# Three W group buffers instead of two in a fused spectral-filter kernel, with the last-stage constants loaded in the drain and six shuffle buffers instead of eight

## The chip, the cores and the metric

The kernel runs on one core of a Trainium2 chip. The metric is device time in microseconds (us), from the start of an execution to its end. Executions of one kernel vary: TensorE's granted clock is halved for stretches whose place and length differ between executions. A run over 1.5% above the fastest run of the same kernel is labelled slow, the others fast. Ratios are the mean time of one kernel's fast runs over the mean of the other's fast runs of the same rounds, so they are not quite the ratio of the medians that are quoted beside them.

Engines: PE is the matrix engine (TensorE), ACT is ScalarE, DVE is VectorE, POOL is GpSimd, SP is SyncE, which here only issues transfers.

## The reference, cut to what matters

```python
def reference(A_x, A_w_r, A_w_i, B_x, B_w_r, B_w_i, gate_w):   # x: 1 x 2048 x 1024, w: 2048 x 513, bf16
    g = sigmoid((A_x * gate_w).sum(-1, keepdims=True))
    X = rfft2(A_x.astype(float32), axes=(-2, -1))
    a = irfft2(X * (A_w_r + 1j * A_w_i), s=(2048, 1024)).astype(bfloat16)
    b = irfft2(X * (B_w_r + 1j * B_w_i), s=(2048, 1024)).astype(bfloat16)    # the kernel uses A_x for both
    return g * a + (1 - g) * b
```

(The B branch is applied to A's x.)

## The kernel before: the parts that matter

The Fourier transforms are matrix products with constant tables. The 2048 rows are handled as 16 "quads" of 128 frequency rows, t = 0 to 15. Four quads share one group of filter weights W (2.1 MB), so there are four groups, loaded into two buffers. Each quad passes a chain over four engines: `f2` (PE, then ACT writes T), `f3` (PE, then ACT writes X), `cmul` (DVE, the product with W, gives Y), `i1` (PE, then ACT writes two tiles rl), and a *shuffle*: one transfer for each rl that lays its rows out anew for the last stage. Two quads, a pair, go through in each turn of the loop.

```python
    wp = ctx.enter_context(tc.tile_pool(name="wp", bufs=2))
    ...
    gw = const.tile([P, 1024], BF16, name="gw")                  # gate weights, read by the 16 gate sums
    ...
    IG = const.tile([P, 8, 512], BF16, name="ig")                # constants of the last stage, 1 MB
    ...
    def load_w(gr):
        w = wp.tile([P, 4, 4, MH], BF16, name="w", tag="w")
        ...  # 16 transfers (20 for group 0) of 128 KB, all on SyncE's queue
    nc.sync.dma_start(WF[:], dr["WF"]); load_w(0); nc.sync.dma_start(WI[:], dr["WI"]); load_w(1)
    nc.sync.dma_start(Ec[:], dr["E"]); nc.sync.dma_start(idb[:], dr["ID"])
    ...
    def zsum(s1):                                                # a gate sum, DVE
        junk = wk.tile([P, 1024], BF16, name="rl", tag="rl", bufs=8)
        nc.vector.scalar_tensor_tensor(out=junk[:], in0=x[:, s1, :], scalar=1.0, in1=gw[:], op0=ALU.mult,
                                       op1=ALU.mult, accum_out=z[:, s1:s1 + 1])
    ...
    def gate_weights(b):
        dg = wk.tile([P, 4, 128], BF16, name="dg", tag="dg", bufs=1)
        nc.gpsimd.tensor_tensor(dg[:], ...)                      # diagonal of gate values, GpSimd
        ...
    for u in range(NT // 2 + 1):
        if 2 * u < NT:
            f2(2 * u)
        if u >= 2:
            i1(2 * u - 4)
        if u >= 1:
            f3(u - 1)
        if 2 * u < NT:
            f2(2 * u + 1)
        if u >= 2:
            i1(2 * u - 3)
        if u >= 1:
            cmul(2 * u - 2)
            cmul(2 * u - 1, ...)
        if u == 2 or u == 4:
            load_w(u // 2 + 1)
        if u == 5:
            nc.sync.dma_start(IG[:], ...)
    ...
    i1(L - 1)                                                    # the drain: quads 14 and 15
    i1(L, (0,))
    i1(L, (1,))                                                  # shuffles of quad 15 go on SyncE's queue
    gate_weights(0)
    spin(24)                                                     # dummy matmuls before the tail
    ...                                                          # the tail: i2_part and i3 for 16 row blocks
```

Of the kernel before, what the change touches and what calls it, by code (L numbers as in the profile page):

```python
# [10 lines left out]
P = 128  # L11
S = 2048
D = 1024
MH = 513
NT = 16
NS1 = 16
BF16 = mybir.dt.bfloat16
# [24 lines left out]
def make_constants():  # L42
# [23 lines left out]
    FD = np.zeros((512, 2, 2, 256))  # L66
    IG = np.zeros((2, 2, 256, 512))
    for eo in range(2):
# [3 lines left out]
        FD[:, eo, 1] = -np.sin(ph)  # L72
        IG[eo, 0] = 2 * np.cos(ph).T
        if eo == 0:
            FD[:, 0, 1, 0] = np.cos(np.pi * d1)
            IG[0, 0, 0] = 1
        m = 2 * i + (2 if eo == 0 else 1)
        IG[eo, 1] = -2 * np.sin(2 * np.pi * np.outer(m, d1) / D)
        if eo == 0:
            IG[0, 1, 255] = np.cos(np.pi * d1)  # L80
    IG /= S * D
    c["FD"] = _bf16np(FD.reshape(4, 128, 2, 512).transpose(1, 2, 0, 3))
# [37 lines left out]
def kernel(ctx, tc, A_x, A_w_r, A_w_i, B_x, B_w_r, B_w_i, gate_w, out):  # L120
    nc = tc.nc
    cn = make_constants()
    dr = {n: nc.inline_tensor(a, name=f"cst_{n.lower()}").ap() for n, a in cn.items()}
# [2 lines left out]

    const = ctx.enter_context(tc.tile_pool(name="const", bufs=1))
    big = ctx.enter_context(tc.tile_pool(name="big", bufs=1))
    wp = ctx.enter_context(tc.tile_pool(name="wp", bufs=2))
    wk = ctx.enter_context(tc.tile_pool(name="wk", bufs=2))  # L130
    yp = tc.alloc_tile_pool(name="yp", bufs=1)
    pp = ctx.enter_context(tc.tile_pool(name="pp", bufs=3, space=bass.MemoryType.PSUM))
# [5 lines left out]
    def ptile():  # L138
        return pp.tile([P, 1024], F32, name="pt", tag="pt")
# [1 line left out]
    ctx.enter_context(tc.manual_schedule())  # L141
    F1 = const.tile([P, 2, 128], BF16, name="f1")
    nc.scalar.dma_start(F1[:].rearrange("p a b -> p (a b)"), dr["F1"])
    gw = const.tile([P, 1024], BF16, name="gw")
    g1 = wk.tile([P, 1024], BF16, name="rl", tag="rl", bufs=8)[0:1, :]
    nc.scalar.dma_start(g1, gate_w.rearrange("(a d) -> a d", a=1))
    ones = const.tile([P, 128], BF16, name="ones")
    nc.vector.memset(ones[:], 1.0)
# [12 lines left out]
    nc.sync.dma_start(FD[:], dr["FD"])  # L161
    WF = const.tile([P, NT, 3, 64], BF16, name="wf")
    WI = const.tile([P, NT, 3, 64], BF16, name="wi")
    IG = const.tile([P, 8, 512], BF16, name="ig")
    Ec = const.tile([P, 2, 128], BF16, name="ec")
    idb = const.tile([P, 128], BF16, name="idb")

# [2 lines left out]
    def load_w(gr):  # L170
        w = wp.tile([P, 4, 4, MH], BF16, name="w", tag="w")
        for a, src in enumerate((A_w_r, A_w_i, B_w_r, B_w_i)):
            for q, r0, dr_ in ((0, 8 * gr, 1), (2, 8 * gr + 4, 1), (1, 64 - 8 * gr, -1), (3, 60 - 8 * gr, -1)):
                c0 = 0
                if gr == 0 and q == 1:
                    nc.sync.dma_start(w[32:64, a, 0, :], bass.AP(src.tensor, 32 * MH, [[64 * MH, 32], [1, MH]]))
                    c0 = 1
                nc.sync.dma_start(w[32 * q:32 * q + 32, a, c0:4, :],  # L178
                                  bass.AP(src.tensor, (r0 + dr_ * c0) * MH, [[64 * MH, 32], [dr_ * MH, 4 - c0], [1, MH]]))
        Ws[gr] = w  # L180
# [8 lines left out]
    ps = ptile()  # L189
# [7 lines left out]
    g = const.tile([P, NS1], F32, name="g")  # L197

    def zsum(s1):
        junk = wk.tile([P, 1024], BF16, name="rl", tag="rl", bufs=8)  # L200
        nc.vector.scalar_tensor_tensor(out=junk[:], in0=x[:, s1, :], scalar=1.0, in1=gw[:], op0=ALU.mult,  # L201
                                       op1=ALU.mult, accum_out=z[:, s1:s1 + 1])

    zs = 0
    for s1 in range(NS1):
        ps = ptile()
        for q in range(4):
            for h in range(2):
                nc.tensor.matmul(ps[:, q * 256:(q + 1) * 256],  # L209
                                 lhsT=x[:, s1, h * 512 + q * 128:h * 512 + (q + 1) * 128],  # L210
                                 rhs=(bc(F1[:, 0, :]).to_broadcast([P, 2, 128]) if h == 0 else F1[:]),
# [28 lines left out]
    Ts, Xs, Ys = {}, {}, {}  # L240
# [12 lines left out]
    def f3(u):  # L253
        ts = (2 * u, 2 * u + 1)
        ps = {t: ptile() for t in ts}
        pl = {t: ps1.tile([P, 512], F32, name=n, tag=n) for t, n in zip(ts, ("pl", "pg"))}
        for r in range(2):
            for e, m in enumerate(((0, 2), (1, 0))[r]):
                for t in ts:
                    for h in range(2):  # L260
                        i_, o_ = slice(64 * h, 64 * h + 64), slice(64 * (h ^ (t & 1)), 64 * (h ^ (t & 1)) + 64)
                        nc.tensor.matmul(ps[t][o_, r * 512 + e:(r + 1) * 512], lhsT=WF[i_, t, m, :],  # L262
                                         rhs=Ts[t][i_, e, e:512], start=(e == 0), stop=(e == 1))
        for r in range(2):
            for t in ts:
                for h in range(2):
                    i_, o_ = slice(64 * h, 64 * h + 64), slice(64 * (h ^ (t & 1)), 64 * (h ^ (t & 1)) + 64)
                    nc.tensor.matmul(pl[t][o_, r:r + 1], lhsT=WF[i_, t, (2, 0)[r], :], rhs=Ts[t][i_, 1, 0:1],
                                     start=(r == 0), stop=(r == 1), skip_group_check=True)
        X = wk.tile([P, 2, 2, MH], BF16, name="X", tag="X")  # L270
        for t in ts:
            nc.scalar.copy(out=X[:, t & 1, :, 0:512], in_=ps[t][:].rearrange("p (r m) -> p r m", r=2))  # L272
            nc.vector.tensor_copy(out=X[:, t & 1, :, 512:513], in_=pl[t][:, 0:2].rearrange("p (r m) -> p r m", m=1))
            Xs[t] = X[:, t & 1]

    def cmul(t, parts=(slice(0, 2),)):
        X, w = Xs.pop(t), Ws[t // 4]
        p = wk.tile([P, 2, 2, MH], BF16, name="p", tag="p", bufs=1)
# [3 lines left out]
        for ab in parts:  # L282
            n = ab.stop - ab.start
            for r, o in ((0, Y), (1, p)):
                nc.vector.tensor_tensor(o[:, ab].rearrange("p a r m -> p (a r) m"),  # L285
                                        bc(X[:, r, :]).to_broadcast([P, 2 * n, MH]),
                                        wv[:, ab].rearrange("p a r m -> p (a r) m"), ALU.mult)
# [3 lines left out]
    def i1(t, parts=(0, 1)):  # L291
        Y = Ys[t]
        ps = {ab: ptile() for ab in parts}
        for e in range(2):
            for r, m in enumerate(((0, 2), (1, 0))[e]):
                for ab in parts:
                    for h in range(2):
                        i_, o_ = slice(64 * h, 64 * h + 64), slice(64 * (h ^ ab), 64 * (h ^ ab) + 64)
                        nc.tensor.matmul(ps[ab][o_, e * 512:(e + 1) * 512], lhsT=WI[i_, t, m, :],  # L299
                                         rhs=Y[i_, ab, r, e:e + 512], start=(r == 0), stop=(r == 1))  # L300
        for ab in parts:
            R = (RA, RB)[ab]
            rl = wk.tile([P, 1024], BF16, name="rl", tag="rl", bufs=8)
            if t == NT - 1 and ab == 1:
                nc.vector.tensor_copy(out=rl[:, 0:512], in_=ps[ab][:, 0:512])
                nc.scalar.copy(out=rl[:, 512:1024], in_=ps[ab][:, 512:1024])
            else:
                nc.scalar.copy(out=rl[:], in_=ps[ab][:])  # L308
            p0 = 32 * ((t // 4) ^ (2 * ab)) + t % 4
            eng = nc.gpsimd if t < NT - 1 else nc.sync  # L310
            eng.dma_start(R[p0:p0 + 29:4, :, :], rl[:])  # L311

    L = NT - 1
# [11 lines that stand above are left out]
        if u >= 1:  # L325
            cmul(2 * u - 2)
            cmul(2 * u - 1, (slice(0, 2),) if 2 * u < NT else (slice(0, 1), slice(1, 2)))
        if u == 2 or u == 4:
            load_w(u // 2 + 1)
        if u == 5:  # L330
            nc.sync.dma_start(IG[:], dr["IG"].rearrange("p a b c d -> p (a b c) d"))
    yp.release()
    tl = ctx.enter_context(tc.tile_pool(name="tl", bufs=4, reuse_waits="tile"))
    EA = tl.tile([P, NS1, 128], BF16, name="ea", tag="ea", bufs=1)
    EB = tl.tile([P, NS1, 128], BF16, name="eb", tag="eb", bufs=1)
    nc.scalar.activation(g[:], z[:], ACT.Sigmoid)
    i1(L - 1)
    i1(L, (0,))
    i1(L, (1,))
    gate_weights(0)  # L340
# [16 lines left out]
    def i3(s1, V):  # L357
        ps = ptile()
        pe = ps[:, 0:512]
        if s1 == NS1 - 1:  # L360
            pe = ps1.tile([P, 512], F32, name="pg", tag="pg")[:]
        for ch in range(8):
            nc.tensor.matmul(pe if ch < 4 else ps[:, 512:1024], lhsT=V[:, ch, :], rhs=IG[:, ch, :],  # L363
                             start=(ch % 4 == 0), stop=(ch % 4 == 3))
        ot = tl.tile([P, 1024], BF16, name="ot", tag="ot")
        ev = tl.tile([P, 512], F32, name="ev", tag="ev")
        nc.scalar.copy(out=ev[:], in_=pe)  # L367
        nc.vector.tensor_tensor(ot[:, 0:512], ev[:], ps[:, 512:1024], ALU.add)  # L368
        nc.vector.tensor_tensor(ot[:, 512:1024], ev[:], ps[:, 512:1024], ALU.subtract)
        nc.sync.dma_start(ov[:, s1, :], ot[:])  # L370
# [8 lines left out]
    for s1 in range(NS1):  # L379
# [3 lines left out]
        if s1 + 3 < NS1:  # L383
            ps = ptile()
# [33 lines left out]
```

## Time and profile before

The time was 159.28 us (median of 6 runs, 158.17 to 163.75). The profiled execution spans 155.8 us.

| stage | us in the profile | what holds it |
|---|---|---|
| x load, first transform | 0 to about 23 | transfers, PE, ACT |
| pair loop | 23 to 94 | ACT, broken by waits for W |
| drain (last pair, last shuffle) | 94 to 108 | a chain through all engines |
| tail | 108 to 156 | PE, without a gap |

The page of the kernel before cuts the span into 40 slices of 3.9 us; a digit is the busy share in tenths, PEclk the granted TensorE clock in tenths, DMA the busy share of the 16 DMA engines.

```profile
DVE  0777999899989979269992987962445763935471
ACT  3277854888999989995999548950666565656530
...
PEclk9999999999999999999999755599999999999999
DMA  5999968899759999999999964355011312223233
```

ACT is at 8 or 9 in the loop (from slice 10) but for slices 19 and 23 to 24, DMA is at 9 from slice 13 to slice 23, and the clock is at half in slices 24 to 26. Now the waits for W. These are lines of DVE's timeline of the kernel before: start, duration, engine, line, operation, output and inputs, and in brackets the idle time just before and what ended it.

```profile
30.84 1.23 DVE L285 TENSOR_TENSOR Y<-X,w 128x2052 bf16<-128x2052 bf16 x1 [0.69 <-ACT X L272]
...
55.64 1.23 DVE L285 TENSOR_TENSOR Y<-X,w 128x2052 bf16<-128x2052 bf16 x1 [0.54 <-ACT X L272]
...
67.45 1.23 DVE L285 TENSOR_TENSOR Y<-X,w 128x2052 bf16<-128x2052 bf16 x1 [3.46 <-DMA w<-in_A_w_r_dram]
...
85.54 1.23 DVE L285 TENSOR_TENSOR Y<-X,w 128x2052 bf16<-128x2052 bf16 x1 [2.40 <-DMA ig<-cst_ig]
```

An ordinary pair's first product waits 0.54 us for its X. That of quad 8 (first of group 2) waits 3.46, that of quad 12 (first of group 3) 2.40. The page puts the second down to IG, but that product does not read IG; the last load of group 3's W landed at 85.36 us, 0.18 us before the product starts, so W is what it waited for. SyncE's timeline of the kernel before tells why they are late (start of the first, time to issue all, count):

```profile
38.75 0.44 SPq L187 DMA_DIRECT2D idb<-cst_id  x1
44.48 2.19 SPq L178 DMA_DIRECT2D w<-in_A_w_r_dram  x4
...
55.85 2.95 SPq L178 DMA_DIRECT2D w<-in_B_w_i_dram  x4
61.65 3.00 SPq L178 DMA_DIRECT2D w<-in_A_w_r_dram  x4
...
78.59 0.38 SPq L331 DMA_DIRECT2D ig<-cst_ig  x1
```

After the last constant (38.75) the queue stands still until 44.48, when group 0's buffer has been read for the last time. The DMA engines are busy for 0.66 of the stretch from 39 to 47 us, and for 0.99 or more in each stretch of a pair from there to 90 us. The last two lines of interest are PE's, around the second wait:

```profile
84.59 1.08 PE L299 MATMUL pt<-Y,wi 64*64 64x512 bf16 x16
88.69 2.09 PE L299 MATMUL pt<-Y,wi 64*64 64x512 bf16 x16 [3.03 <-DVE Y L288]
```

The sixteen matmuls of one quad take 2.09 us after the gap of 3.03 and 1.08 before it. The clock record of the trace has the half clock from 87.7 to 101.3 us.

### The profile page before, as it was taken

To read this page: it belongs to the slowest core of one execution; us is meant where nothing else is said; L and a number is where in the kernel's file an instruction comes from. 1 tells how busy PE (TensorE), PEld (TensorE's weight loads), DVE (VectorE), ACT (ScalarE), POOL (GpSimd) and SP (SyncE) were. 2 spreads that over 40 slices of the span, in tenths; PEclk is the share of its full clock that TensorE was granted. 3 is DMA by queue.
4 is the path that set the end of the run, shared out by engine and by line. 5 is a ranking of instruction groups with operands and counts; after the bars stand their busy time and mean duration, and the time that the engine had idled before them with its cause. 6 is when DMAs were issued, how large, how long until landed. Compare 5 with 4: busy or idle time off the path is not lost.

```text
span 155.8 us, 2909 instructions
## 1 busy us (share of the span) xinstructions
PE 127.5 (82%) x1138; PEld 70.9 (46%) x1138; DVE 111.0 (71%) x166; ACT 106.0 (68%) x112; POOL 22.4 (14%) x38
## 2 busy tenths in 40 slices
PE   6999959987878788955879286855999999999980
PEld 5568844433333333412324032315675656566530
DVE  0777999899989979269992987962445763935471
ACT  3277854888999989995999548950666565656530
POOL 0000000003140413331133320370200200000000
PEclk9999999999999999999999755599999999999999
DMA  5999968899759999999999964355011312223233
GB/s 164 277 411 429 353 153 234 296 246 256 198 123 188 250 231 231 229 230 228 215 223 255 233 225 123 89 144 182 0 72 67 135 67 113 94 85 119 79 127 137
DMA packets 14993, 29.24 MB, mean 188 GB/s; under 512 B 4097, under 2 KB 8449, under 8 KB 14338
## 3 DMA queue, kind: packets, MB, share of 16 engines
q1 hardware_dynamic: 10512, 21.09, 46.3%
q0 software_dynamic: 4320, 7.88, 21.4%
q8 instruction: 9, 0.15, 0.4%
q10 hardware_dynamic: 146, 0.07, 0.2%
q14 instruction: 6, 0.05, 0.1%
HBM read 16.44 MB, written 4.19 MB: 132 GB/s over the span
## 4 chain that ended last, share of the span: by engine, by line
PE 38%; DMA 32%; DVE 11%; ACT 8%; issue 4%; SPq 3%; DVEq 0%; ACTq 0%
PE pt L363 17%; DMA w<-in_B_w_i_dram 10%; PE pt L349 9%; DMA w<-in_A_w_i_dram 7%; DMA w<-in_A_w_r_dram 6%; DMA xr<-in_A_x_dram 6%; PE pt L209 5%; DVE Y L285 4%; DVE p L285 3%; PE pt L246 3%; DMA xr<-rl 3%; SPq L178 3%; ACT rl L308 3%; ACT y L221 2%; ACT X L272 2%
## 5 line engine op out<-in xcount | busy, mean ns | idle before, releaser
L308 ACT CAST rl<-pt 128x1024 bf16<-128x1024 f32 x31 | 29.9, 1021 | 6.3 <-issue 3.0
L246 PE MATMUL pt<-fd,y 128*128 128x512 bf16 x128 | 29.8, 379 | 4.7 <-ACT T L249 2.9
L299 PE MATMUL pt<-Y,wi 64*64 64x512 bf16 x256 | 22.8, 435 | 7.9 <-DVE Y L288 7.0
L363 PE MATMUL pt<-ig,V 128*128 128x512 bf16 x124 | 29.2, 379 | 0.0
L249 ACT CAST T<-pt 128x1024 bf16<-128x1024 f32 x16 | 20.9, 1308 | 7.5 <-PE pt L246 7.5
L285 DVE TENSOR_TENSOR Y<-X,w 128x2052 bf16<-128x2052 bf16 (+1 forms) x17 | 19.8, 1165 | 8.3 <-DMA w<-in_A_w_r_dram 4.0
L354 ACT CAST V<-pt 128x1024 bf16<-128x1024 f32 x16 | 16.0, 1014 | 9.9 <-PE pt L349 9.9
L368 DVE TENSOR_TENSOR ot<-ev,pt 128x512 bf16<-128x512 f32 x16 | 11.0, 687 | 15.9 <-ACT ev L367 15.9
L311 POOL DMA_DIRECT2D xr<-rl x15 | 9.1, 608 | 79.6 <-ACT rl L308 43.2
L246 PEld LDWEIGHTS <-y 128*128 128x128 bf16 x128 | 11.9, 97 | 19.0 <-issue 6.9
L285 DVE TENSOR_TENSOR p<-X,w 128x2052 bf16<-128x2052 bf16 (+1 forms) x17 | 19.7, 1160 | 0.0
L201 DVE SCALAR_TENSOR_TENSOR rl<-xr,gw 128x1024 bf16<-128x1024 bf16 x16 | 18.7, 1220 | 0.0
L299 PEld LDWEIGHTS <-wi 64*64 64x64 bf16 x256 | 8.1, 114 | 21.0 <-DVE Y L288 9.9
L363 PEld LDWEIGHTS <-V 128*128 128x128 bf16 x128 | 12.0, 98 | 12.4 <-ACT V L354 0.3
L262 PE MATMUL pt<-T,wf 64*64 64x511 bf16 (+1 forms) x128 | 12.4, 412 | 6.2 <-ACT rl L308 4.4
L209 PE MATMUL pt<-f_78,xr 128*128 128x256 bf16 x128 | 16.5, 295 | 0.3
L221 ACT CAST y<-pt 128x1024 bf16<-128x1024 f32 x13 | 12.5, 1022 | 6.2 <-PE pt L209 6.0
L367 ACT COPY ev<-pt 128x512 f32<-128x512 f32 x15 | 8.8, 586 | 10.8 <-PE pt L363 10.8
L272 ACT CAST X<-pt 128x1024 bf16<-128x1024 f32 x16 | 15.4, 1020 | 0.9 <-ACT rl L308 0.7
L209 PEld LDWEIGHTS <-xr 128*128 128x128 bf16 x128 | 13.2, 105 | 4.2 <-DMA xr<-in_A_x_dram 1.9
L288 DVE TENSOR_TENSOR Y<-Y,p 128x1026 bf16<-128x1026 bf16 (+1 forms) x17 | 11.4, 668 | 0.6
L289 DVE TENSOR_TENSOR Y<-Y,p 128x1026 bf16<-128x1026 bf16 (+1 forms) x17 | 11.1, 656 | 0.0
(37 smaller groups left out, 103.1 us busy)
## 6 DMA issues: line engine op xcount, KB each, us to landing
out_dram<-ot SPq DMA_DIRECT2D x16, 256.0 KB, 2.0
xr<-rl POOLq DMA_DIRECT2D x15, 256.0 KB, 9.2
rb<-rl POOLq DMA_DIRECT2D x15, 256.0 KB, 9.1
xr<-in_A_x_dram SPq DMA_DIRECT2D x3, 1024.0 KB, 10.6
w<-in_A_w_r_dram SPq DMA_DIRECT2D x15, 128.2 KB, 6.5
w<-in_A_w_i_dram SPq DMA_DIRECT2D x15, 128.2 KB, 8.3
w<-in_B_w_r_dram SPq DMA_DIRECT2D x15, 128.2 KB, 5.0
w<-in_B_w_i_dram SPq DMA_DIRECT2D x15, 128.2 KB, 7.8
```

What stands on the lines that cost most here:

```text
L201: nc.vector.scalar_tensor_tensor(out=junk[:], in0=x[:, s1, :], scalar=1.0, in1=gw[:], op0=ALU.mult, op1=ALU.mult, accum_out=z[:, s1:s1 + 1])
L209: nc.tensor.matmul(ps[:, q * 256:(q + 1) * 256], lhsT=x[:, s1, h * 512 + q * 128:h * 512 + (q + 1) * 128], rhs=(bc(F1[:, 0, :]).to_broadca ...
L221: nc.scalar.copy(out=o, in_=i_)
L246: nc.tensor.matmul(ps[:, eo * 512:(eo + 1) * 512], lhsT=y[:, q, eo, 2 * t:2 * t + 2].rearrange("p h a b -> p (h a b)"), rhs=FD[:, eo, q, : ...
L249: nc.scalar.copy(out=T[:].rearrange("p e (i o) -> p o e i", o=2), in_=ps[:].rearrange("p (o e i) -> p o e i", o=2, e=2))
L272: nc.scalar.copy(out=X[:, t & 1, :, 0:512], in_=ps[t][:].rearrange("p (r m) -> p r m", r=2))
L285: nc.vector.tensor_tensor(o[:, ab].rearrange("p a r m -> p (a r) m"), bc(X[:, r, :]).to_broadcast([P, 2 * n, MH]), wv[:, ab].rearrange("p ...
L299: nc.tensor.matmul(ps[ab][o_, e * 512:(e + 1) * 512], lhsT=WI[i_, t, m, :], rhs=Y[i_, ab, r, e:e + 512], start=(r == 0), stop=(r == 1))
L308: nc.scalar.copy(out=rl[:], in_=ps[ab][:])
L349: nc.tensor.matmul(ps[:, ch * 128:(ch + 1) * 128], lhsT=R[:, s1, c0:c0 + 255:2], rhs=Ew[:, s1, :], start=(ab == 0 and ch % 4 == 0), stop=( ...
L354: nc.scalar.copy(out=V[:].rearrange("p c s -> p (c s)"), in_=ps[:])
L363: nc.tensor.matmul(pe if ch < 4 else ps[:, 512:1024], lhsT=V[:, ch, :], rhs=IG[:, ch, :], start=(ch % 4 == 0), stop=(ch % 4 == 3))
```

## The change

The intent: with a third buffer group 2 need not wait for group 0's, nor group 3 for group 1's, so both load sooner. SBUF was full, so room had to be made: IG moves out of its own tile into two halves in buffers of Y that are free in the drain, gw moves into one of the three buffers of T, rl goes from eight to six buffers, X is allocated per quad.

```diff
-    wp = ctx.enter_context(tc.tile_pool(name="wp", bufs=2))
+    wp = ctx.enter_context(tc.tile_pool(name="wp", bufs=3))
-    gw = const.tile([P, 1024], BF16, name="gw")
-    g1 = wk.tile([P, 1024], BF16, name="rl", tag="rl", bufs=8)[0:1, :]
+    gw = wk.tile([P, 1024], BF16, name="T", tag="T", bufs=3)
+    g1 = wk.tile([P, 1024], BF16, name="rl", tag="rl", bufs=6)[0:1, :]
-    IG = const.tile([P, 8, 512], BF16, name="ig")
 ...   (rl: bufs=6 wherever it is allocated; X: one tile per quad, bufs=3)
-        if u == 2 or u == 4:
-            load_w(u // 2 + 1)
-        if u == 5:
-            nc.sync.dma_start(IG[:], ...)
+        if u == 0 or u == 2:
+            load_w(u // 2 + 2)
+    def load_ig():
+        i = len(IG)
+        IG.append(wk.tile([P, 4, 512], BF16, name="Y", tag="Y", bufs=3))
+        nc.sync.dma_start(IG[i][:], ...[:, 4 * i:4 * i + 4])
+    load_ig()
     i1(L - 1)
+    load_ig()
     i1(L, (0,))
     i1(L, (1,))
```

More of the change, by code (lines that the diff above doesn't have):

```diff
@@ L199, in zsum @@
     def zsum(s1):
-        junk = wk.tile([P, 1024], BF16, name="rl", tag="rl", bufs=8)
+        junk = wk.tile([P, 1024], BF16, name="rl", tag="rl", bufs=6)
         nc.vector.scalar_tensor_tensor(out=junk[:], in0=x[:, s1, :], scalar=1.0, in1=gw[:], op0=ALU.mult,
@@ L269, in f3 @@
                                      start=(r == 0), stop=(r == 1), skip_group_check=True)
-        X = wk.tile([P, 2, 2, MH], BF16, name="X", tag="X")
         for t in ts:
-            nc.scalar.copy(out=X[:, t & 1, :, 0:512], in_=ps[t][:].rearrange("p (r m) -> p r m", r=2))
-            nc.vector.tensor_copy(out=X[:, t & 1, :, 512:513], in_=pl[t][:, 0:2].rearrange("p (r m) -> p r m", m=1))
-            Xs[t] = X[:, t & 1]
+            X = wk.tile([P, 2, MH], BF16, name="X", tag="X", bufs=3)
+            nc.scalar.copy(out=X[:, :, 0:512], in_=ps[t][:].rearrange("p (r m) -> p r m", r=2))
+            nc.vector.tensor_copy(out=X[:, :, 512:513], in_=pl[t][:, 0:2].rearrange("p (r m) -> p r m", m=1))
+            Xs[t] = X
     def cmul(t, parts=(slice(0, 2),)):
@@ L302, in i1 @@
             R = (RA, RB)[ab]
-            rl = wk.tile([P, 1024], BF16, name="rl", tag="rl", bufs=8)
+            rl = wk.tile([P, 1024], BF16, name="rl", tag="rl", bufs=6)
             if t == NT - 1 and ab == 1:
@@ L327 @@
             cmul(2 * u - 1, (slice(0, 2),) if 2 * u < NT else (slice(0, 1), slice(1, 2)))
-        if u == 2 or u == 4:
-            load_w(u // 2 + 1)
-        if u == 5:
-            nc.sync.dma_start(IG[:], dr["IG"].rearrange("p a b c d -> p (a b c) d"))
+        if u == 0 or u == 2:
+            load_w(u // 2 + 2)
     yp.release()
@@ L336 @@
     nc.scalar.activation(g[:], z[:], ACT.Sigmoid)
+    IG = []
+    def load_ig():
+        i = len(IG)
+        IG.append(wk.tile([P, 4, 512], BF16, name="Y", tag="Y", bufs=3))
+        nc.sync.dma_start(IG[i][:], dr["IG"].rearrange("p a b c d -> p (a b c) d")[:, 4 * i:4 * i + 4])
+    load_ig()
     i1(L - 1)
+    load_ig()
     i1(L, (0,))
@@ L362, in i3 @@
         for ch in range(8):
-            nc.tensor.matmul(pe if ch < 4 else ps[:, 512:1024], lhsT=V[:, ch, :], rhs=IG[:, ch, :],
+            nc.tensor.matmul(pe if ch < 4 else ps[:, 512:1024], lhsT=V[:, ch, :], rhs=IG[ch // 4][:, ch % 4, :],
                              start=(ch % 4 == 0), stop=(ch % 4 == 3))
```

## The prediction

> **What bounds the kernel now.** The chain of waits runs through three regimes. Until about 30 us: the x load and the first transform. From 30 to 102 us: a software pipeline over eight pairs of quads; there ScalarE is nearly full (in the timeline one pair costs it 2 x 1.31 us for T, 2 x 1.02 for X, 4 x 1.02 for rl = 8.8 us minus overlaps, and pairs come 8.6 us apart) and VectorE is second (7.5 us a pair). From 108 us: a PE-bound tail, 45 us with PE gapless, which the change leaves alone.
>
> The pipeline is broken twice by W. In VectorE's timeline the first product of group 2 starts at 67.45 us after 3.46 us idle (its X was ready at 64.5), and that of group 3 at 85.54 us after 2.40 us idle (named ig, X ready at 83.7). The SyncE timeline shows why: group 2's loads are issued only at 44.48, when group 0's last product reading W ends, and take until about 67; group 3's start at 61.65, and the 1 MB IG load (issued 78.6, 12.3 us to landing) shares the DMA with its end. The DMA row is at 99-108% from 47 to 90 us, but only 66% from 39 to 47.
>
> The second wait costs more than itself. PE idles 3.03 us before the matmuls of quad 12, and the granted clock falls to 0.5 from about 87.7 to 101.3 us; quad 12's sixteen inverse matmuls then take 2.09 us, against 1.08 before. The Trainium skill, "TensorE: Matmul & The Clock Gate", What's actually happening, says that idle windows bring the half clock back; this trace agrees, though the drop came after only 2.0 us of that gap.
>
> **What the change does.**
> 1. Group 2 is issued right after the identity, about 39.2 instead of 44.5, and should land near 62; group 3 follows without the wait, landing near 78. Needed at about 66 and 83: both W waits go.
> 2. IG leaves the contended stretch and loads as two 512 KB halves at about 93 and 97 us, where DMA is half idle; needed at 107. Perhaps 0.3 us on the last shuffles (the second half is on their queue).
> 3. The cost: gw now lives in a T buffer. The third T (28.61 us now) must wait for the last gate sum, which ends at 29.99. X0, the first product and the whole ScalarE-bound pipeline start 1.4 us later.
> 4. Six rl buffers: reuse comes three quads later, 11.9 to 14 us. Write, issue and a shuffle of 9.2 us median need 10.5 to 11.5. Tight: a latency over 10.6 us would stall ScalarE. I allow 0.2 us. Single X tiles: nothing.
>
> **Sum.** Group 2's product starts at 66.0 instead of 67.45, but ScalarE gains only 0.4 there. Group 3's product starts at 83.2 instead of 85.5 (-2.3). The PE gap shrinks from 3.0 to about 1.1 us, so quad 12 and the last f3 should run at full clock: 1.0 and 0.7 us more, so the last X is some 4.0 us earlier. The half clock may still come in the drain's next gap. Less 0.5 for items 2 and 4: -3.6 us.
>
> Predicted 155.7 us, range 153.6 to 158.2. Faster by over 2%: 0.58; within 2%: 0.39; slower: 0.03.
>
> **Signs.** No DMA wait before any product; the third T starting near 30.0 and the first product near 32.3; the tail's first matmul near 104.5 instead of 108.2; full clock at quad 12; rl never waiting for a shuffle.
>
> **What would make it wrong.** The half clock staying in the drain anyway (then about -2), or falling into the tail; shuffles of over 10.6 us stalling rl; IG delaying the last shuffle; group 2 landing after 66.

## The result

The changed kernel takes 155.39 us (median of 10 runs, 154.05 to 160.93) against 158.22 us for the kernel before (median of 20 runs, the six of before and those taken with the measurement of the change). The ratio of the fast runs is 0.9841 (95% interval 0.9792 to 0.9891), about 2.5 us. The prediction was 155.7 us. The interval crosses the line of 2%; the profiled execution spans 152.1 us and is a fast one.

The same rows of the changed kernel's page (slices of 3.8 us):

```profile
DVE  0879999589997979798797999640463944936381
ACT  3298836588999999998999897610965556656530
...
PEclk9999999999999999999999997869999999999998
DMA  5999967899899999999985369981012213222233
```

ACT has no break before slice 25. DMA runs at 9 from slice 12 to slice 20, has a hole in slices 22 to 24, and is full again in 25 to 27, where the two halves of IG and the last shuffles meet. The clock is at 7, 8 and 6 in slices 25 to 27, two short stretches of half clock. DVE's first products of the pairs, in the changed kernel:

```profile
31.05 1.23 DVE L284 TENSOR_TENSOR Y<-X,w 128x2052 bf16<-128x2052 bf16 x1 [2.15 <-ACT X L271]
...
55.74 1.23 DVE L284 TENSOR_TENSOR Y<-X,w 128x2052 bf16<-128x2052 bf16 x1 [0.54 <-ACT X L271]
...
64.28 1.23 DVE L284 TENSOR_TENSOR Y<-X,w 128x2052 bf16<-128x2052 bf16 x1 [0.54 <-ACT X L271]
...
81.67 1.23 DVE L284 TENSOR_TENSOR Y<-X,w 128x2052 bf16<-128x2052 bf16 x1 [0.54 <-ACT X L271]
```

Quads 8 and 12 wait 0.54 us for their X, as quad 6 does. SyncE's queue:

```profile
38.34 0.99 SPq L186 DMA_DIRECT2D idb<-cst_id  x1
39.38 2.73 SPq L177 DMA_DIRECT2D w<-in_A_w_r_dram  x4
...
47.71 4.16 SPq L177 DMA_DIRECT2D w<-in_B_w_i_dram  x4
52.48 4.71 SPq L177 DMA_DIRECT2D w<-in_A_w_r_dram  x4
...
65.80 3.97 SPq L177 DMA_DIRECT2D w<-in_B_w_i_dram  x4
90.46 4.55 SPq L339 DMA_DIRECT2D Y<-cst_ig  x2
```

Group 2 follows the last constant at once (39.38), group 3 at 52.48, all of W is issued by 69.8 instead of at 78.5. PE at quad 12:

```profile
82.58 1.08 PE L298 MATMUL pt<-Y,wi 64*64 64x512 bf16 x16
84.83 1.44 PE L298 MATMUL pt<-Y,wi 64*64 64x512 bf16 x16 [1.17 <-DVE Y L287]
```

The gap is 1.17 us and the matmuls run at full clock (1.44 us includes waiting for the second half of Y). Here is the cost that the change brought at the start, in ACT's timeline, the second and third T of the changed kernel and then of the kernel before:

```profile
25.63 1.32 ACT L248 CAST T<-pt 128x1024 bf16<-128x1024 f32 x1 [0.41 <-PE pt L245]
28.84 1.29 ACT L248 CAST T<-pt 128x1024 bf16<-128x1024 f32 x1 [1.90 <-DVE X L272]
...
71.17 1.01 ACT L307 CAST rl<-pt 128x1024 bf16<-128x1024 f32 x1 [0.35 <-DMA rb<-rl]
```

```profile
26.88 1.31 ACT L249 CAST T<-pt 128x1024 bf16<-128x1024 f32 x1 [0.41 <-PE pt L246]
28.61 1.32 ACT L249 CAST T<-pt 128x1024 bf16<-128x1024 f32 x1 [0.41 <-PE pt L246]
```

The third T waits 1.90 us for DVE, which is reading gw in the T buffer that it needs, instead of 0.41 for PE. (The line names the small copy into X that DVE runs right behind its last gate sum; that gate sum ends at 28.75 us, and the third T starts at 28.84.) The rl line is the one place where six buffers were too few in this execution: 0.35 us. And the end of the drain, SyncE's last A shuffle and PE's first matmul of the tail, of the kernel before and the changed one:

```profile
102.82 0.80 SPq L311 DMA_DIRECT2D xr<-rl  x1
```

```profile
108.23 1.50 PE L349 MATMUL pt<-ea,xr 128*128 128x128 bf16 x24 [1.06 <-DMA xr<-rl]
```

```profile
97.75 0.81 SPq L310 DMA_DIRECT2D xr<-rl  x1
```

```profile
104.65 1.50 PE L355 MATMUL pt<-ea,xr 128*128 128x128 bf16 x24 [1.46 <-DMA xr<-rl]
```

From issue to first use it was 5.41 us before (108.23 - 102.82) and is 6.90 now (104.65 - 97.75).

One correction is needed before these traces are compared: in the changed kernel's profiled execution the second stage began 1.25 us sooner (first `f2` matmul at 21.98 instead of 23.23), before anything that the change touches could matter. In e1 and e9 below, the same program, it was 22.35 and 22.63, and in e5, the kernel before with fillers, 22.64; this start varies. Measured from that matmul:

| event, us after the first f2 matmul | before | changed | difference |
|---|---|---|---|
| third T starts | 5.38 | 6.86 | +1.48 |
| first product of quad 8 | 44.22 | 42.30 | -1.92 |
| first product of quad 12 | 62.31 | 59.69 | -2.62 |
| last pair's X | 70.28 | 66.32 | -3.96 |
| last A shuffle issued | 79.59 | 75.77 | -3.82 |
| first matmul of the tail | 85.00 | 82.67 | -2.33 |
| end | 132.55 | 130.12 | -2.43 |

So 4 us were won by the last pair, and 1.5 of them were lost in the last shuffle. The end agrees with the ratio of the timed runs (2.5 us). But each column is one execution: the same program had its last X at 69.48 in e1 and at 66.66 in e9.

### The profile page after: what moved, and what is told of

The parts are those of the page before. It is cut to its first block, busy times and chain, and to the rows that moved or that the text cites. A ratio compares the mean times of both kernels' runs of the same rounds, so it can differ in the third digit from the quotient of the medians.

```text
span 152.1 us, 2910 instructions
## 1 busy us (share of the span) xinstructions
PE 125.5 (82%) x1138; PEld 71.3 (47%) x1138; DVE 110.9 (73%) x166; ACT 105.7 (69%) x112; POOL 22.5 (15%) x38
## 4 chain that ended last, share of the span: by engine, by line
PE 44%; DVE 19%; DMA 13%; ACT 11%; issue 7%; POOL 2%; DVEq 0%; ACTq 0%; POOLq 0%
PE pt L369 18%; PE pt L355 10%; DVE rl L200 9%; DMA rb<-rl 7%; PE pt L245 6%; ACT rl L307 5%; PE pt L208 5%; DMA xr<-rl 4%; ACT T L248 4%; DVE Y L284 3%; DVE p L284 3%; DVE y L218 2%; PE pt L261 2%; ACT X L271 2%; PE pt L298 2%
## 5 line engine op out<-in xcount | busy, mean ns | idle before, releaser
L369 PE MATMUL pt<-Y,V 128*128 128x512 bf16 x124 | 29.2, 379 | 0.0
L298 PE MATMUL pt<-Y,wi 64*64 64x512 bf16 x256 | 20.8, 402 | 5.0 <-DVE Y L287 4.1
L200 DVE SCALAR_TENSOR_TENSOR rl<-xr,T 128x1024 bf16<-128x1024 bf16 x16 | 18.6, 1222 | 0.0
L261 PE MATMUL pt<-T,wf 64*64 64x512 bf16 (+1 forms) x128 | 11.2, 381 | 6.5 <-ACT rl L307 4.2
L208 PE MATMUL pt<-f_78,xr 128*128 128x256 bf16 x128 | 15.8, 290 | 0.0
L298 PEld LDWEIGHTS <-wi 64*64 64x64 bf16 x256 | 7.5, 109 | 17.2 <-issue 7.2
```

The lines of the kernel that those rows point to most:

```text
L208: nc.tensor.matmul(ps[:, q * 256:(q + 1) * 256], lhsT=x[:, s1, h * 512 + q * 128:h * 512 + (q + 1) * 128], rhs=(bc(F1[:, 0, :]).to_broadca ...
L261: nc.tensor.matmul(ps[t][o_, r * 512 + e:(r + 1) * 512], lhsT=WF[i_, t, m, :], rhs=Ts[t][i_, e, e:512], start=(e == 0), stop=(e == 1))
L298: nc.tensor.matmul(ps[ab][o_, e * 512:(e + 1) * 512], lhsT=WI[i_, t, m, :], rhs=Y[i_, ab, r, e:e + 512], start=(r == 0), stop=(r == 1))
L369: nc.tensor.matmul(pe if ch < 4 else ps[:, 512:1024], lhsT=V[:, ch, :], rhs=IG[ch // 4][:, ch % 4, :], start=(ch % 4 == 0), stop=(ch % 4 = ...
```

## The experiments

Twelve runs; all gave a correct result. The kernel before ran as well, on the same chip. The table has the medians of all runs of a kernel, fast and slow; the ratio uses the fast ones alone.

| run | what differs from the changed kernel | median (range), us | kernel before | ratio to it, 95% |
|---|---|---|---|---|
| e1 | nothing | 156.69 (155.17 to 157.35) | 157.84 | 1.007, 0.995 to 1.018 |
| e2 | gw in p | 154.95 (154.27 to 158.37) | 157.84 | 0.997, 0.989 to 1.005 |
| e3 | IG into a freed W buffer | 158.15 (154.12 to 161.82) | 157.84 | 1.001, 0.978 to 1.024 |
| e4 | e2 and e3 | 154.21 (151.69 to 159.36) | 157.84 | 0.986, 0.970 to 1.001 |
| e5 | kernel before with PE fillers | 160.23 (155.79 to 161.42) | 156.50 | none (one fast run) |
| e6 | PE fillers | 156.59 (154.87 to 157.45) | 156.50 | 0.992, 0.985 to 0.999 |
| e7 | PE fillers, gw in p | 156.09 (153.09 to 161.00) | 156.50 | 0.977, 0.969 to 0.985 |
| e8 | e7, second IG half last | 155.74 (154.11 to 158.12) | 156.50 | 0.986, 0.979 to 0.993 |
| e9 | W loads at their old places in the text | 154.89 (154.02 to 155.05) | 157.07 | 0.986, 0.980 to 0.992 |
| e10 | gw in p, first dg on DVE | 155.91 (152.54 to 159.36) | 157.07 | 0.977, 0.966 to 0.987 |
| e11 | e10, second IG half last | 155.77 (153.83 to 157.94) | 157.07 | 0.987, 0.979 to 0.995 |
| e12 | two W buffers | 158.87 (156.76 to 163.42) | 158.60 | 1.006, 0.992 to 1.021 |

The ratios of the first call look poor because the kernel before had four lucky runs there (154.09 to 155.96), which alone count as its fast ones; seven of its eleven runs were above 157. The times scatter so much that most of what follows rests on stages of the traces, and on times only where they are clear.

### e1: the changed kernel again

No edit.

> The changed kernel again, unaltered, so that the others of this call have it on the same chip. Theory: about 2.5 us under the kernel before (ratio 0.984), as the first measurement gave (0.979 to 0.989). Profile: third T released by the last gate sum, no W wait, a last shuffle of about 6.8 us with the second IG half in flight.

Its median was 1.15 us under that of the kernel before, the fast runs no better than its lucky ones. The trace held the surprise:

```profile
67.35 1.23 DVE L284 TENSOR_TENSOR Y<-X,w 128x2052 bf16<-128x2052 bf16 x1 [3.24 <-DMA w<-in_A_w_r_dram]
```

The same kernel waits for W at quad 8 after all, 3.24 us, nearly as long as the kernel before. In this execution group 2's loads were issued from 40.79 to 58.5 us, in the one above from 39.38 to 51.9. Between 44 and 52 us the DMA engines moved 1.80 and 1.87 MB in the two, hardly different, but SyncE's queue had 0.89 MB of it here and 0.99 there, the shuffles 0.91 and 0.88. So the two kinds of transfers divide the same engines, and W's margin (in the profile of the result group 2 landed 4.44 us and group 3 2.25 us before its first product) is not safe. The Trainium skill, "DMA: Bandwidth & Descriptors", Queues, rings and completion order, says that each DMA engine takes turns between the queues that have work, a packet at a time; the near-even split here agrees with it. What tips the split from one execution to the next no run here shows. Over the eleven profiles with three W buffers, DVE was idle for 1.3 us or more before the product of quad 8 in four (e1, e7, e8, e11), and there the issue of group 2's loads ended at 56.1 us or later; in the other seven it ended by 55.2 us, and the wait was 0.54 us. In three of the four (e7, e8, e11) the product of quad 12 waited for group 3 as well, 2.76, 2.36 and 3.06 us. Each of these products, whatever the page names as its releaser, started 0.17 or 0.18 us after its group's last load landed. The delay was there before group 2: the last load of group 1 landed at 45.3 to 47.5 us in these four, at 40.4 to 45.1 in the other seven. Three of the four are slow runs.

### e2: gw in the product buffer

```diff
-    gw = wk.tile([P, 1024], BF16, name="T", tag="T", bufs=3)
+    gw = wk.tile([P, 2052], BF16, name="p", tag="p", bufs=1)[:, 0:1024]
```

> Only gw moves: from a T buffer to the single product buffer p, which VectorE alone writes, so nothing else waits for it. Theory (the late third T costs its 1.4 to 1.5 us in full): the third T starts 1.7 us after the second T again and the run is 1.3 to 1.5 us faster than the changed kernel. Rival (the delay is absorbed further on, by the pipeline catching up): under 0.4 us faster.

The third T starts 5.38 us after the first f2 matmul, as before the change. The median fell by 1.74 us against e1 and the fast runs by 1.1% (mean of four, 154.69, over that of six, 156.40). But this is not clean evidence for the 1.4 to 1.5 us: e1's profile contains a W wait, and in e2's profile part of the head start was lost again, 0.5 us at the first product, which now came right after the last load of group 0 had landed (30.4 us), and more a pair later, when ACT idled for 0.68 and 1.02 us as a half clock of 3.4 us came at 36.3. The line of that first product:

```profile
30.71 1.23 DVE L284 TENSOR_TENSOR Y<-X,w 128x2052 bf16<-128x2052 bf16 x1 [1.18 <-DMA w<-in_B_w_i_dram]
```

Four more profiles with gw in p are like it (e4, e7, e8, e11). In these five the first product came 8.09 to 8.66 us after the first f2 matmul, each time about 0.3 us after group 0's last load landed, against 9.07 in the changed kernel and 7.60 in the kernel before. So the third T is early in all of them, but only 0.4 to 1.0 of its 1.5 us reached the first product; the next thing to hold it was group 0's W (the page names W in four of the five, ACT's X in e7). In one profile of the six, e10 below, group 0 landed early enough (28.58 us).

### e3 and e4: IG in a freed W buffer, without and with e2

```diff
+        if u == 6:
+            igb = wp.tile([P, 16 * MH], BF16, name="w", tag="w")
+            IG = igb[:, 0:4096].rearrange("p (c d) -> p c d", d=512)
+            nc.sync.dma_start(IG, ...)
```

(and the two `load_ig()` calls are gone)

> Only IG moves: one 1 MB load into the W buffer that group 1 has freed, issued right after group 3's loads (about 70 us), instead of two halves in the drain. Theory (the second half delays the last shuffle): issue to landing of the last shuffle is back from 6.8 to about 5.3 us and the run is 1.2 to 1.6 us faster than the changed kernel, less what the load costs shuffles at 70 to 80 us (rl waits up to 0.5 us). Rival (the last shuffle is slow for another reason, quad 14's shuffle just ahead of it): still 6.5 us or more, no gain.

> Both. Theory: the two lie one after the other on the chain, so they add: 2.5 to 3.0 us faster than the changed kernel, 5 us or more under the kernel before (ratio about 0.966). Rival: one hides the other, no better than the better one alone.

Both had slow profiles. e3 alone gave no gain. e4 did better than its ratio suggests: its median was 2.48 us under that of e1, which is the 2.5 expected against the changed kernel, and 3.63 under that of the kernel before, not the 5 expected; the intervals of the two ratios overlap, and e2's own 1.74 is part of it, so what IG's place gave stays unclear. In e3 the load of 1 MB, put in just behind W, did the harm that six rl buffers cannot take; ACT's timeline of e3:

```profile
82.56 1.01 ACT L307 CAST rl<-pt 128x1024 bf16<-128x1024 f32 x1 [2.83 <-DMA rb<-rl]
```

ACT waited 2.83 us for a shuffle to give its rl buffer back, against 0.35 in the changed kernel (in e4 1.21 and 0.29). That fits why the change moves IG out of the loop: with six buffers that stretch has no room for it (e7 had a wait of 0.79 us there even without IG). In e4 the last A shuffle took 6.10 us from issue to first use, with no IG near it; so not all of the 6.9 is IG's.

### e5 to e8: fillers on PE

```diff
         if 2 * u < NT:
+            if u >= 2:
+                spin(4)
             f2(2 * u)
         if u >= 2:
+            spin(10 if 2 * u == NT else 0)
             i1(2 * u - 4)
         if u >= 1:
+            if u >= 2:
+                spin(5)
             f3(u - 1)
 ...
+    spin(20)
     i1(L - 1)
```

e5 is the kernel before with this, e6 the changed kernel, e7 has gw in p too, and e8 also issues the second half of IG after `i1(L, (1,))`.

> The kernel before, with dummy 128x128 matmuls of ones put where PE idles in the pair loop and in the drain (4 and 5 a pair, 10 and 20 in the drain; results unchanged). Theory (a random half clock, brought on by PE idling, makes the spread between runs and a part of what the W waits cost): spread of the six runs under 2 us instead of 4 to 6, mean granted clock 0.97 or more, median 1 to 2 us under the kernel before. Rival (the spread comes from elsewhere, such as the DMA): spread and median as before, whatever the clock. If the fillers delay PE's own work, the median rises.

> The changed kernel with the same fillers. Theory: against e5 of this call the change is worth 1 to 2.5 us with the clock held (W waits of 3.3 and 2.1 us gone, 1.45 us lost to the late third T, about 1 us to the last shuffle). Rival (the gain was only the clock): no difference from e5.

> e6 with gw in the product buffer p instead of a T buffer. Theory: 1.3 to 1.5 us faster than e6. Rival (absorbed further on): under 0.5 us.

> e7 with the second IG half issued behind the last two shuffles of the same queue instead of ahead of them. Theory (that half delays the last shuffle): issue of the last A shuffle to the tail's first matmul falls from 6.7-6.9 to about 5.4-6.0 us, and the run is about 1 us faster than e7. Rival: unchanged last shuffle, or the tail now waits for IG.

The expectation failed in its main part: the spread did not shrink (e5: 155.79 to 161.42), and the medians did not fall. The fillers kept the full clock through quads 12 to 14 in the profiles of e5, e6 and e8, but in all four the half clock then came at about 100 us, in the last matmuls of the drain and the dummy matmuls before the tail. e6 against e5 has the sign of the theory (3.6 us between the medians, and 0.9 between their fastest runs), with so much scatter that no size follows. e7 against e6 shows 0.5 us between the medians and 1.8 between the fastest runs. e8 shows nothing of IG: its tail waited for the dummy matmuls at half clock, not for a shuffle (the profiles of e7 and e8 are of slow runs). e5's profile waits for W at both quads, as the kernel before does: 2.13 us at quad 8, 2.29 at quad 12.

What these runs did show is a second thing that differs between executions. DVE and then POOL of e6, at the last product:

```profile
96.58 0.43 DVE L289 TENSOR_TENSOR Y<-Y,p 128x513 bf16<-128x513 bf16 x1
96.92 1.63 DVE L290 TENSOR_TENSOR Y<-Y,p 128x513 bf16<-128x513 bf16 x1
```

```profile
97.21 1.05 POOL L232 TENSOR_TENSOR dg<-idb,g 128x512 bf16<-128x512 bf16 x1
```

The last product takes 1.63 us instead of 0.42, and POOL computes dg during that time. In the profiles up to here it was so five times in ten (e3, e5, e6, e7, e8), always with dg starting while the product was being worked on; in the other five dg started after its end and it took 0.42. The Trainium skill, "SBUF — State Buffer", Who interferes with whom, says that a DVE instruction with two SBUF inputs contends with a GpSimd instruction that reads SBUF, and that issue order decides which of the two blocks. The trace agrees that they contend; by the recorded starts it was the earlier one, DVE's, that was stretched, by 1.21 us, about the length of dg (1.05).

### e9: W loads at their old places

```diff
-        if u == 0 or u == 2:
-            load_w(u // 2 + 2)
+        if u == 2 or u == 4:
+            load_w(u // 2 + 1)
```

> The changed kernel with only the W loads put back to their old places (group 2 after the third pair, group 3 after the fifth), all else changed as it is. Theory (the gain is the earlier W): VectorE waits for W again before the products of quads 8 and 12 (about 2 us and 1 to 2 us, a little less than before because IG no longer shares that stretch), the third T stays late, and the run is no faster than the kernel before, 2 to 3 us slower than the changed kernel. Rival (the gain is IG out of the W stretch): no wait at quad 12, under 1 us slower than the changed kernel.

No W wait came back, and the ratio was 0.986, close to the 0.984 of the changed kernel. The test was void: SyncE has nothing else to issue in between, so the order and the waits of its queue are the same to the instruction in both texts, as a comparison of the two builds showed afterwards. So e9 is a repetition of the changed kernel, and one finding: of the change's two edits to the W loads, moving them in the text does nothing; only the third buffer can matter.

### e10 and e11: the gate diagonal on DVE, and IG behind the shuffles

```diff
-        nc.gpsimd.tensor_tensor(dg[:], ...)          # in gate_weights(0)
+    dg0 = gate_dg(0, nc.vector)                      # between i1(L, (0,)) and i1(L, (1,))
     i1(L, (1,))
+    load_ig()                                        # e11 only, in place of the one before i1(L, (0,))
+    gate_weights(0, dg0)
```

Both also have gw in p.

> e2 (gw in p) and the first gate diagonal dg moved from GpSimd to VectorE, right behind the last product. In five of the ten profiles so far the last product took 1.63 us instead of 0.42, each time with GpSimd's dg starting while it ran. Theory (the two block each other): the last product takes 0.42 us in this profile and dg under 0.8 us; median about 0.6 us under e2 of the first call, and with a narrower spread. Rival (the long product has another cause, such as the last shuffle's writes): 1.6 us still appears.

> e10 with the second IG half issued behind the last two shuffles. Theory (that half, just ahead of the last A shuffle on its queue, delays it): issue of that shuffle to the tail's first matmul falls from 6.7-6.9 us (e10 should show that again) to 5.4-6.0, and the run is 0.8 to 1.4 us faster than e10. Rival: the same 6.5 us or more, so the half is innocent; or the first matmuls on IG wait for it at about 108 us.

DVE's first product in e10, and the end of its product chain:

```profile
30.23 1.23 DVE L289 TENSOR_TENSOR Y<-X,w 128x2052 bf16<-128x2052 bf16 x1 [0.69 <-ACT X L276]
...
95.53 0.42 DVE L293 TENSOR_TENSOR Y<-Y,p 128x513 bf16<-128x513 bf16 x1
95.86 0.68 DVE L230 TENSOR_TENSOR dg<-idb,g 128x512 bf16<-128x512 bf16 x1
```

The product is short in both, and dg costs 0.68 us in a stretch where DVE would have waited for PE. That supports the theory: 1.63 us did not appear in either, though two profiles, where half had it, prove little alone. The spread did not narrow (152.54 to 159.36), so this was not its main cause; and the median is 0.96 us above e2's instead of under it, on another chip. As an expectation of times it failed.

e10's profile is also the one of six that shows gw undisturbed: from the first f2 matmul its third T starts at 5.38 us, its first product at 7.61 as in the kernel before (9.07 in the changed one), and its last X comes at 64.56 instead of 66.32, 1.76 us sooner: about the late third T in full, and the 0.35 us of rl wait that it did not have. In the other fast profile with gw in p, e2, the last X came at 66.55, no sooner than in the changed kernel, so what gw in p brings depends on the execution.

In e11, whose profile is of a slow run, W was late again (a wait of 3.06 us at quad 12). Its last A shuffle was done within 5.51 us, the time to the first use, which did not wait for it. But the B shuffle, now with IG close behind it, was waited for:

```profile
110.04 1.50 PE L361 MATMUL pt<-eb,rb 128*128 128x128 bf16 x24 [1.21 <-DMA rb<-rl]
```

It was issued at 103.90, so 6.1 us. The half of IG had moved from one shuffle to the other, and the ratio was no better than e10's. So where A waited on the transfer, A's time from issue to first use was 6.90, 6.66, 6.90, 7.49, 6.58, 6.55 and 5.56 us with the second half ahead of it (changed kernel, e1, e2, e6, e9, e10, e12; mean 6.7) and 5.41 and 6.10 without IG in the drain (before, e4; mean 5.8). The first group had the DMA engines busy for 0.85 to 0.99 of the 5.4 us after A's issue, the second for 0.55 and 0.57. IG in the drain costs the last shuffle about 0.9 us on average, 1.5 and more in single executions; with two profiles in one group this size is rough.

### e12: two W buffers, all else changed

```diff
-    wp = ctx.enter_context(tc.tile_pool(name="wp", bufs=3))
+    wp = ctx.enter_context(tc.tile_pool(name="wp", bufs=2))
```

(with the loads at their old places, which e9 showed to be without effect where there are three buffers)

> e9 was no test: with three buffers the queue's order and waits are the same wherever the loads stand in the text. Here the changed kernel has two W buffers again and nothing else of it is undone, so group 2 waits for group 0's buffer and group 3 for group 1's. Theory (the earlier W is the gain): group 2's first load is issued near 45 instead of 39 us, the product of quad 8 waits 2 us or more and that of quad 12 1 us or more, the third T is late as well, and the run is not faster than the kernel before (ratio 0.995 to 1.015), about 2.5 us slower than the changed kernel. Rival (moving IG out of the W stretch, not the third buffer, is the gain): no wait at quad 12 and a ratio under 0.99.

```profile
67.29 1.23 DVE L284 TENSOR_TENSOR Y<-X,w 128x2052 bf16<-128x2052 bf16 x1 [2.43 <-DMA w<-in_A_w_r_dram]
...
84.59 1.23 DVE L284 TENSOR_TENSOR Y<-X,w 128x2052 bf16<-128x2052 bf16 x1 [1.62 <-DMA w<-in_B_w_i_dram]
```

```profile
37.44 0.37 SPq L186 DMA_DIRECT2D idb<-cst_id  x1
45.82 2.31 SPq L177 DMA_DIRECT2D w<-in_A_w_r_dram  x4
...
74.45 2.10 SPq L177 DMA_DIRECT2D w<-in_B_w_i_dram  x4
```

Both waits are back (2.43 and 1.62 us), the queue stands still from 37.8 to 45.82, and the ratio is 1.006: the other edits of the change, without the third buffer, gain nothing and perhaps cost a little. e9, the changed kernel to the instruction, had 0.986 on the same chip. That is the answer to the rival: moving IG out of the loop is not the gain (at quad 12 the wait is 1.62 with IG out of the loop and 2.40 with it there, one profile each), the third buffer is. From 1.006 to 0.986 is about 3 us, but the two intervals meet at 0.992, so the size is rough. The stages say the same: measured from the first f2 matmul, e12's last X comes at 69.33 us, against 66.32 and 66.66 in the profile of the result and in e9. All three profiles with two buffers (the kernel before, e5, e12) wait for W at both quads; of the eleven with three, six wait at neither, and e3's wait at quad 12 is for the rl buffer.

The best ratio of all is that of e10 (and of e7), 0.977. It rests on two fast runs of six in each, because one or two lucky runs moved the border; between the medians of all runs e10 is 1.16 us and e7 0.41 under the kernel before. Their intervals (0.966 to 0.987, 0.969 to 0.985) cross the line of 2%, and that either beats the changed kernel is not shown.

## Why the prediction was right, and where it was off

The predicted 155.7 us met 155.39, and the chain of causes held, but for one term, point by point:

- **The W waits go (item 1).** Right in the profile of the result (0.54 us at both quads), and e12 shows the third buffer to be the cause. But the margin was overrated: the prediction had group 2 land near 62, four before it is needed; four of the eleven profiles with three buffers waited for it again, three of them at quad 12 as well.
- **The late third T (item 3).** Predicted 1.4 us, measured 1.48 at the third T and 1.47 at the first product. Taking it away gave it all back in e10 alone; in the five other profiles with gw in p, group 0's W took a part. It was found by asking which buffer each tile takes over and who reads that one last.
- **The gap on PE and the clock (sum).** Predicted 1.1 us and full clock for quad 12, measured 1.17 and 1.44 us for its matmuls. That the half clock would come in a later gap was named as possible and happened (93.0 to 96.4 and 99.8 to 103.2 us). Predicted for the last X -4.0 us, measured -3.96. That this is so close is luck: by the same measure e9 gives -3.62 and e1, with its W wait, -0.80.
- **Six rl buffers (item 4).** Predicted 0.2 us, measured 0.35 at one place (the sign that rl never waits was missed there). In e3, where shuffles took longer, 2.83: the buffers are just enough for this order of loads.
- **IG in the drain (item 2).** This is the term of the sum that was mis-sized: "Perhaps 0.3 us on the last shuffles". In the profile of the result the last shuffle lost 1.5 us (6.90 against 5.41), over the profiles about 0.9. The prediction saw that the second half sits on the shuffle's queue, and took the DMA engines for "half idle", but read that from the kernel before, where IG was not there: with IG they are busy for 0.96 of the last 10 us before 100. With it the sum would have been -2.4, which is what came (-2.5 by the ratio). That the median came within 0.3 us of the number is luck: the gain was taken about 1 us too large (3.6 against 2.5), and the base of 159.28, from six runs, was 1 us above the median of the twenty, and the two cancel. So is the tail's first matmul, predicted near 104.5 and found at 104.65: the profiled execution started its second stage 1.25 us sooner, without which it would have been near 105.9.

As for the chances: it gave 0.58 to "faster by over 2%", and the measured ratio of 0.984 leans to within 2%. The overlooked part of the shuffle and the executions with a late W explain that side.

What stays open: what tips the split of the DMA engines between W and shuffles, and what brings the half clock to one place or another. Neither the fillers nor dg on DVE narrowed the spread.

## What to carry to other kernels

Give a queue a free buffer and it loads as early as its order allows; the place of the load in the program text is worth nothing where that queue has no other work (e9), the wait for the buffer everything (e12). When room is made by letting tiles share buffers, ask for each shared buffer who reads it last and who wants it first: a tile parked in the buffers of a critical producer held that producer up by 1.5 us here, and not at all in a buffer that only the tile's own reader writes; how much of that reaches the end depends on what is next to hold the chain (here often group 0's W). And when a load is moved into a stretch that looked idle, count the transfer on the critical path that runs in that stretch with the load beside it, not as it ran alone.

## What the Trainium skill lacked or had wrong

- "SBUF — State Buffer", Who interferes with whom: right that the two instructions contend, but it has issue order decide which one blocks, so the first should run on. Here (e6) DVE's product began at 96.92 us, GpSimd's dg at 97.21, and it was the product that took 1.63 us instead of 0.42 while dg kept its 1.05 (GpSimd's recorded times are rough, so the order may be less certain than the size).
- "TensorE: Matmul & The Clock Gate", What's actually happening: an idle window of about 3.4 us brings the half clock. Here it came 2.0 us into a gap of 3.03, and in another execution (e2, 36.3 us) in a loop whose longest gaps were about 1 us; in the 3.41 us before, PE had been busy for 1.38 and 1.54 us, so the window need not be idle throughout. The lengths do fit the page's window: 3.4, 6.8, 10.2 and 13.7 us. It lacks how much work keeps the full clock.
- "DMA: Bandwidth & Descriptors", Queues, rings and completion order: the even split in bytes is in line with taking turns, but it has no number for transfers within SBUF beside loads. A shuffle of 256 KB took 4.1 to 5.1 us with little beside it (kernel before, from 92 us) and 8.8 to 11.2 beside W (changed kernel, 45 to 70 us).
- No page that was consulted says that two executions of one kernel can divide the same DMA bandwidth differently: 0.99 and 0.89 MB for the loads in the same 8 us; the second execution went on to wait 3.24 us for W.

